# Strassen's seven products for the two bilinear projections: quarters of w_a and w_b, eight of nine token tiles

## The chip, the cores and the metric

The kernel runs on one core of a Trainium2 chip. The metric is the device time of one execution in microseconds (us). The engines are PE (TensorE: matmuls; PEld is its loading of stationary operands), DVE (VectorE), ACT (ScalarE), POOL (GpSimd) and SP (SyncE, which here only issues DMAs). Matmuls read SBUF and write PSUM, eight banks of 128 x 512 fp32.

## The reference

Attention with a forgetting bias is followed by a mixture of eight experts and by a bilinear layer:

```
x = attention(q, k, v, s)                      # 1152 tokens x 512
P = sinkhorn(x @ w_gate)                       # 1152 x 8
y = sum_e P[:, e] * (relu(x @ w1[e]) @ w2[e])  # 512 -> 1024 -> 512, for 8 experts
a = y @ w_a;  b = y @ w_b                      # 512 -> 1536, both
out = (a * b) @ w_out                          # 1536 -> 512
```

Every matmul of the experts and of the bilinear layer is made of three fp16 matmuls: both operands are split into a high and a low fp16 part, and high x high, high x low and low x high are summed in PSUM. The inputs of the bilinear layer's weights come as fp64 and are turned into fp32 on the chip.

## The kernel before, in words

Tokens come in nine tiles of 128, in the order of the list `ORDER`. Attention is interleaved with expert 0. Then experts 1 to 7 follow. For experts 2 to 7 the first product is done by Strassen's scheme with seven products of quarters (`h_seven`): `x_sums` makes four sums of quarters of the activations once, `w_sums` makes the four sums of quarters of the weights for each expert, and the products go through PSUM banks X (`mb` 0 and 1), Y (`yb` 2 and 3), Z (`yb` 4) and A (`mb` 2), with additions on DVE and copies on ACT. The second product of an expert (`y_tile`, lines 1041 to 1043) goes tile by tile, 24 matmuls with 512 moving columns each, into `yb` 0 and 1; DVE adds the result to `acc` (line 1439).

While the experts run, `m2_prep` makes fp16 pairs of the bilinear layer's weights, in pieces of 1 MB of fp64 (18 pieces, six of each weight): a DMA into the tile `mr`, six DVE instructions that turn fp64 into fp32 (lines 1205 to 1213, into `h`), a maximum over the tile (ACT, POOL), then the high part (ACT, line 358) and the low part (DVE, line 372). Two pieces fill one buffer `wun6`, which `m2_out` writes to DRAM. `M2N` says how many such pairs of pieces are made in each expert's stage: 0, 1, 1, 1, 2, 2, 2 for experts 1 to 7. `m2_in` reads the finished buffers back when they are needed.

With the last expert, `xm_split` follows each tile of y: an absolute sum on ACT (line 1452), five small DVE instructions for the scale, the high part on ACT (line 358), the low part on DVE (line 372), and a transposing DMA into `xt` (line 1456). Then come the products with w_a and w_b: `ab_block` takes three tiles (384 columns) at a time, for each of 12 blocks of 128 of the 1536 features and for each of the two weights 12 matmuls (lines 1485 to 1487: four blocks of the 512 inputs by three). ACT copies a with its scale (line 1493), DVE multiplies b into it (line 1496), ACT and DVE split the product into two fp16 parts (lines 1498, 1499). `out_block` makes the last product tile by tile (lines 1525 to 1527). The first `ab_block` stands ahead of the last three tiles of y:

```
for p in range(NTL):
    if last and p == 2 * BT:
        ab_block(0)
    y_tile(e, p, xm_split if last else None)
```

The order of instructions on each engine is made by a list scheduler (`Graph.schedule`) out of written costs, latencies and ranks. Each engine then works through its list in order.

Of the kernel before, what the change touches and what calls it, by code (L numbers as in the profile page):

```python
# [246 lines left out]
def forgetting_attention_moe_bilinear_kernel(  # L247
# [25 lines left out]
    BT = 3  # L273
# [821 lines left out]
    th = []  # L1095

    def switch():
# [8 lines left out]
        for i in range(2):  # L1106
# [4 lines left out]
            big["a", i] = big["ts", i][:, DM:DM + BN]  # L1111
# [3 lines left out]
        for buf, n in ((big["sx"].rearrange("p i z c t -> p (i z c t)"), 3), (big["ht"].rearrange("p z f t -> p (z f t)"), 6)):  # L1115
            for i in range(n):
                th.append(buf[:, i * 8 * BN:(i + 1) * 8 * BN].rearrange("p (z f t) -> p z f t", z=2, f=4))
# [75 lines left out]

    def m2_prep(wi, pc, un, rank):
        if wi < 2:
            a = (w_a, w_b)[wi][:, pc * 256:(pc + 1) * 256]
        else:
            a = w_out[pc * 256:(pc + 1) * 256, :]
        src = a.bitcast(I32).rearrange("(c p) f -> p c f", p=128)
        nch = 4 if wi < 2 else 2  # L1200
# [3 lines left out]
        g.add("SP", 2913, lambda: nc.sync.dma_start(out=stage[2].bitcast(I32).rearrange("p (c f) -> p c f", c=nch), in_=src), r=["hold"], w=sk, rank=rank)  # L1204
# [16 lines left out]
        if wi < 2:  # L1221
            fo = (pc % 2) * 256
            part = lambda zz: units[un][:, zz, :, fo:fo + 256]
            cs = range(4)
        else:
            co = (pc % 2) * 2
            part = lambda zz: units[un][:, zz, co:co + 2]
            cs = range(co, co + 2)
        src2 = cf.rearrange("p (c f) -> p c f", c=nch)
        g.add("ACT", 1145, lambda: hi_of(part(0), src2, sx), r=h0k[1] + [key], w=[("u", un, 0, c, pc % 2) for c in cs], rank=rank)  # L1230
        uk = [("u", un, zz, c) for zz in range(2) for c in range(4)]
        ok = [("u", un, zz, c, pc % 2) for zz in range(2) for c in cs]
# [414 lines left out]
```

## Time and profile before

| | before |
|---|---|
| time, median of 3 runs | 1077.06 us (1074.89 to 1078.08) |
| the profiled execution: its own time | 1076.89 us |
| its span, first to last instruction | 1075.1 us |
| PE busy | 1023.1 us, 95% |
| DVE busy | 655.8 us, 61% |
| ACT busy | 487.8 us, 45% |
| POOL busy | 156.3 us, 15% |

The span is what the trace covers; the execution's own time is 1.8 us longer. A busy share is a mean over stages with different limits, so a change is costed in the stages that it touches. Durations of matmuls overlap (they are pipelined); what a stream of them takes is the step from one start to the next.

### The profile page before, as it was taken

The numbers are of one execution on the slowest core, as the hardware profiler recorded it, in microseconds if no ns is written. First come the engines' busy times: TensorE is split into PE (matmuls) and PEld (weight loads), VectorE is DVE, ScalarE is ACT, GpSimd is POOL, SyncE is SP. The second block draws the span as 40 slices with busy tenths as digits, with TensorE's granted clock in tenths as the row PEclk, the third lists the DMA queues.
The fourth block names the chain that finished last, engine by engine and source line by source line (L and its number), as shares of the span: only waits on it lengthen the run. The fifth ranks groups of instructions, "written<-read, shape, count | busy, mean of one in ns | idle before, by whom it ended". The sixth has DMA issues, their size and how long they took to land.

```text
span 1075.1 us, 18959 instructions
## 1 busy us (share of the span) xinstructions
PE 1023.1 (95%) x7811; PEld 645.8 (60%) x7811; DVE 655.8 (61%) x1361; ACT 487.8 (45%) x920; POOL 156.3 (15%) x192
## 2 busy tenths in 40 slices
PE   1598999999999999999999999999999999999998
PEld 0476777766546745754764774674575564565565
DVE  7885773149975873883793698789668723121221
ACT  4686576246525543652562654553544422021120
POOL 3876666120000000000000000000000000000000
PEclk9899999999999999999999999999999999999999
DMA  9894851011123132221403324413327503100000
GB/s 235 178 184 83 159 81 22 1 51 64 54 79 118 40 118 70 89 71 47 154 4 118 119 64 171 158 40 144 139 110 253 159 1 98 40 1 10 21 1 30
DMA packets 114998, 96.17 MB, mean 89 GB/s; under 512 B 87248, under 2 KB 87504, under 8 KB 112608
## 3 DMA queue, kind: packets, MB, share of 16 engines
q1 hardware_dynamic: 113856, 94.68, 30.3%
q8 instruction: 61, 1.00, 0.4%
q10 hardware_dynamic: 1056, 0.28, 0.1%
q14 instruction: 25, 0.20, 0.1%
HBM read 69.00 MB, written 11.80 MB: 75 GB/s over the span
## 4 chain that ended last, share of the span: by engine, by line
PE 90%; DVE 6%; POOL 2%; issue 1%; DMA 0%; ACT 0%; DVEq 0%; POOLq 0%
PE yb L1041 10%; PE yb L1043 10%; PE yb L1042 10%; PE yb L1381 4%; PE yb L1383 4%; PE yb L1382 4%; PE mb L1485 4%; PE mb L1487 4%; PE mb L1486 4%; PE mb L1381 3%; PE mb L1382 3%; PE mb L1383 3%; PE yb L1526 2%; PE yb L1527 2%; PE yb L1525 2%
## 5 line engine op out<-in xcount | busy, mean ns | idle before, releaser
L1041 PE MATMUL yb<-wun,ht 128*128 128x512 f16 x504 | 191.1, 379 | 0.0
L1042 PE MATMUL yb<-wun,ht 128*128 128x512 f16 x504 | 191.1, 379 | 0.0
L1043 PE MATMUL yb<-wun,ht 128*128 128x512 f16 x504 | 191.1, 379 | 0.0
L1439 DVE SCALAR_TENSOR_TENSOR acc<-yb,pe,acc 128x512 f32<-128x512 f32 x63 | 47.2, 750 | 86.3 <-PE yb L1043 85.0
L358 ACT ACTIVATE wun<-stage,sc 128x1024 f16<-128x1024 f32 (+1 forms) x58 | 60.1, 1054 | 78.4 <-PE yb L1043 71.0
L372 DVE SCALAR_TENSOR_TENSOR wun<-stage,sc,wun 128x1024 f16<-128x1024 f32 (+1 forms) x66 | 80.1, 1231 | 15.7 <-ACT wun L358 15.6
L1043 PEld LDWEIGHTS <-ht 128*128 128x128 f16 x504 | 49.3, 98 | 59.5
L1042 PEld LDWEIGHTS <-ht 128*128 128x128 f16 x504 | 49.3, 98 | 57.3 <-issue 0.3
L1041 PEld LDWEIGHTS <-ht 128*128 128x128 f16 x504 | 49.3, 98 | 57.1
L1381 PE MATMUL yb<-sx,wun 128*128 128x288 f16 x288 | 82.4, 286 | 0.6 <-DVE yb L1396 0.6
L1382 PE MATMUL yb<-sx,wun 128*128 128x288 f16 x288 | 82.4, 286 | 0.0
L1383 PE MATMUL yb<-sx,wun 128*128 128x288 f16 x288 | 82.4, 286 | 0.0
L1382 PEld LDWEIGHTS <-wun 128*128 128x128 f16 x672 | 65.7, 98 | 19.5 <-issue 0.7
L1381 PEld LDWEIGHTS <-wun 128*128 128x128 f16 x672 | 65.7, 98 | 18.8
L1383 PEld LDWEIGHTS <-wun 128*128 128x128 f16 x672 | 65.7, 98 | 16.6
L1496 DVE TENSOR_TENSOR ts<-mb,ts 128x384 f32<-128x384 f32 x36 | 20.1, 557 | 76.8 <-PE mb L1487 76.8
L355 ACT ACTIVATE jk<-stage 128x1024 f16<-128x1024 f32 x52 | 54.7, 1053 | 23.7 <-DMA stage<-in_moe_w_dram 23.2
L1485 PE MATMUL mb<-xt,wun 128*128 128x384 f16 x192 | 62.6, 326 | 0.0
L1487 PE MATMUL mb<-xt,wun 128*128 128x384 f16 x192 | 62.6, 326 | 0.0
L1486 PE MATMUL mb<-xt,wun 128*128 128x384 f16 x192 | 62.6, 326 | 0.0
L897 POOL TENSOR_TENSOR pt<-p,pt 128x512 f16<-128x512 f32 (+1 forms) x46 | 55.0, 1198 | 25.1 <-ACT pt L894 19.8
L1391 ACT ACTIVATE ht<-yb 128x288 f16<-128x288 f32 x96 | 39.0, 407 | 39.1 <-PE yb L1383 37.7
(305 smaller groups left out, 2582.8 us busy)
## 6 DMA issues: line engine op xcount, KB each, us to landing
stage<-in_moe_w_dram SPq DMA_DIRECT2D x26, 1024.0 KB, 5.0
md<-wun SPq DMA_DIRECT2D x9, 1024.0 KB, 3.8
wun<-md SPq DMA_DIRECT2D x7, 1024.0 KB, 6.2
stage<-in_moe_w_dram SPq DMA_DIRECT2D x24, 256.0 KB, 4.3
mr<-in_moe_w_a_dram SPq DMA_DIRECT2D x6, 1024.0 KB, 6.1
mr<-in_moe_w_b_dram SPq DMA_DIRECT2D x6, 1024.0 KB, 5.3
mr<-in_moe_w_out_dram SPq DMA_DIRECT2D x6, 1024.0 KB, 6.0
stage<-md SPq DMA_DIRECT2D x2, 1024.0 KB, 4.8
```

The source lines that it names most:

```text
L358: nc.scalar.activation(hi, src, AF.Copy, scale=scale)
L372: eng.scalar_tensor_tensor(out=lo, in0=src, scalar=scale, in1=hi, op0=ALU.mult, op1=ALU.subtract)
L897: lambda hi=hi, lo=lo, src=src: nc.gpsimd.tensor_tensor(out=lo, in0=src, in1=hi, op=ALU.subtract)),
L1041: nc.tensor.matmul(pp, lhsT=hh, rhs=wh, start=(f == 0), stop=False)
L1042: nc.tensor.matmul(pp, lhsT=hh, rhs=wl, start=False, stop=False)
L1043: nc.tensor.matmul(pp, lhsT=hl, rhs=wh, start=False, stop=(f == KF - 1))
L1381: nc.tensor.matmul(p, lhsT=wh, rhs=xh, start=first and ch == 0, stop=False, skip_group_check=True)
L1382: nc.tensor.matmul(p, lhsT=wh, rhs=xl, start=False, stop=False, skip_group_check=True)
L1383: nc.tensor.matmul(p, lhsT=wl, rhs=xh, start=False, stop=ch == 1, skip_group_check=True)
L1485: nc.tensor.matmul(p, lhsT=wh, rhs=xh, start=(c == 0), stop=False)
L1486: nc.tensor.matmul(p, lhsT=wh, rhs=xl, start=False, stop=False)
L1487: nc.tensor.matmul(p, lhsT=wl, rhs=xh, start=False, stop=(c == KD - 1))
```

## The change

The products with w_a and w_b are regrouped. The 1536 features are handled as six pairs of blocks, j and j + 6. Tile 0 of `ORDER` keeps plain products (`ab_plain`, 128 moving columns). The other eight tiles are two halves of 512 columns, and for each pair of blocks and each weight seven products of quarters stand where there were eight (`ab_seven`). The sums of quarters of the activations are made by `x2_sums` for a tile of each half at a time, into the space of `acc`; the sums of quarters of the weights are made in `m2_prep` beside the quarters themselves, so that a piece of w_a or w_b (one pair of blocks) now fills a whole `wun6`. In DRAM there are 15 such buffers in place of 9. A pair of blocks of w_a and the same of w_b make one entry of the list of preparations (six such entries, then three of w_out), and `M2N` is 0, 2, 1, 2, 1, 2, 1. With the last expert y goes through the tiles in another order, the products with w_a and w_b come behind all of y, and all `out_tile`s behind them.

```diff
@@ m2_prep, for a piece of w_a or w_b
-        g.add("SP", 2913, lambda: nc.sync.dma_start(out=stage[2].bitcast(I32).rearrange("p (c f) -> p c f", c=nch), in_=src), r=["hold"], w=sk, rank=rank)
+            for h in range(2):
+                g.add("SP", 1457, lambda h=h: nc.sync.dma_start(out=dst_()[h], in_=src[h]), r=["hold"] + ([("sth", 0)] if h else []),
...
+            tsum(T[0], qd[:, 0, 1], qd[:, 0, 0])
+            tsum(T[1], qd[:, 1, 1], qd[:, 0, 1])
+            tsum(T[2], qd[:, 1, 1], T[0])
+            tsum(T[3], qd[:, 1, 0], T[2])
+            g.add("ACT", 1145, lambda: hi_of(plain[0](), src2, sx), r=h0k[1] + [key], w=uk(0, 0), rank=rank)
+            g.add("DVE", 1300, lambda: lo_of(nc.vector, plain[1](), src2, sx, plain[0]()), r=h0k[1] + [key] + uk(0, 0), w=uk(1, 0), rank=rank)
+            g.add("ACT", 1145, lambda: hi_of(uv(0)[:, 1024:2048], uf, sx), r=h0k[0] + [key], w=uk(0, 1), rank=rank)
+            g.add("DVE", 1300, lambda: lo_of(nc.vector, uv(1)[:, 1024:2048], uf, sx, uv(0)[:, 1024:2048]), r=h0k[0] + [key] + uk(0, 1), w=uk(1, 1), rank=rank)
...
@@ new: sums of the activations' quarters, for one tile of each half
+    def x2_sums(kk):
...
+        def tt(out, a, b, op, r, w):
+            g.add("DVE", 400, lambda: nc.vector.tensor_tensor(out=out(), in0=a(), in1=b(), op=op), r=r, w=w, rank=rk)
+        def split(i, src, keys):
+            hi, lo = (lambda: accs[:, 4 + kk, i]), (lambda: accs[:, kk, i])
+            g.add("ACT", 400, lambda: nc.scalar.activation(hi(), src(), AF.Copy), r=keys, w=[("S", kk, i, 0)], rank=rk)
+            tt(lo, src, hi, ALU.subtract, keys + [("S", kk, i, 0)], [("S", kk, i, 1)])
...
@@ new: tile 0, plain
+    def ab_plain(j):
...
+                for h in range(2):
+                    p = yb[z][:, h * 128:(h + 1) * 128]
                     for c in range(KD):
...
+                        wh, wl = (wt[:, y, 2 * h + c // 2, c % 2] for y in range(2))
+                        xh, xl = (xt[:, y, c, 0:128] for y in range(2))
...
@@ new: the other eight tiles
+    def ab_seven(j):
+        plain = lambda r, t: (lambda z, c: xt[:, z, 2 * r + c, T0 + t * TN:T0 + (t + 1) * TN])
+        summed = lambda i: (lambda z, c: accs[:, 4 * (1 - z):4 * (1 - z) + 4, i, c])
...
+        for c in range(2):
+            prod(5, c, A, ak, True)
+            act_copy(S5[c], A, ak, [("s5m", c)])
+            prod(1, c, X[c], xbk[c], True)
+            act_copy(Y[c], X[c], xbk[c], yk[c])
+        for c in range(2):
+            prod(2, c, X[c], xbk[c], False)
+            out(c, X[c], xbk[c], 0, 0)
+            prod(6, c, Y[c], yk[c], False)
+            dve_add(Z, Y[c], S5[c], yk[c] + [("s5m", c)], zk)
+            prod(7, c, Y[c], yk[c], False)
+            dve_add(W[c], Y[c], S5[c], yk[c] + [("s5m", c)], [("wm", c)])
+            prod(3, c, Z, zk, False)
+            out(c, Z, zk, 1, 0)
+            prod(4, c, Y[c], yk[c], False)
+            out(c, Y[c], yk[c], 0, 1)
+            out(c, W[c], [("wm", c)], 1, 1)
...
@@ the end of the program
-    m2q = [(wi, x) for wi in range(3) for x in range(NP2 // 2)]
+    m2q = [((0, x), (1, x)) for x in range(FH)] + [((2, x),) for x in range(NP2 // 2)]
...
-        for p in range(NTL):
-            if last and p == 2 * BT:
-                ab_block(0)
+        for p in (0, 1, 5, 2, 6, 3, 7, 4, 8) if last else range(NTL):
             y_tile(e, p, xm_split if last else None)
-    nyb[0] = 5
+            if last and p > 4:
+                x2_sums(p - 5)
...
+    for j in range(3):
+        ab_plain(j)
+    for j in range(3):
+        ab_seven(j)
+        for wi in range(2):
+            m2_in(wi, 3 + j, w2r[wi, j], [], prank())
     for i in range(2):
         m2_in(2, 1 + i, 2 + i, [("u", 2 + i, z, c) for z in range(2) for c in range(4)], prank())
-    out_block(0)
-    ab_block(1)
-    out_block(1)
-    ab_block(2)
-    out_block(2)
+    for j in range(3, FH):
+        ab_plain(j)
+        ab_seven(j)
+    nyb[0] = 5
+    for p in range(NTL):
+        out_tile(p)
...
-M2N = (0, 1, 1, 1, 2, 2, 2)
+M2N = (0, 2, 1, 2, 1, 2, 1)
```

A product (`prod`) is six matmuls of 512 moving columns (two blocks of inputs by three); the index c there is the weight, a or b. For products 3, 5, 6 and 7 the moving operand is read from `accs` as four pieces of 128 columns.

What the scheduler makes of this is seen on DVE at two places. The first is behind the last tile of y of the last expert. Before, DVE has there the addition into `acc` (line 1439), the scale's small instructions and the low part (line 372) that the transposing DMA waits for:

```order
L1439 SCALAR_TENSOR_TENSOR acc_72<-yb1_3545,pe_66,acc_72 128x512
L338 TENSOR_SCALAR sc_63<-sc_63 128x1
L339 TENSOR_SCALAR sc_63<-sc_63 128x1
L342 TENSOR_SCALAR sc_63<-sc_63 128x1
L343 TENSOR_SCALAR sc_63<-sc_63 128x1
L345 TENSOR_SCALAR sc_63<-sc_63 128x1
L1508 TENSOR_SCALAR sc_63<-sc_63 128x1
L372 SCALAR_TENSOR_TENSOR ts1_3537<-acc_72,sc_63,ts1_3537 128x512
```

In the changed kernel the same chain (the addition is line 1451 there, the rest as before) has sums of `x2_sums` for the pair of tiles ahead (line 1496) and the first plain product's multiplication (line 1552) among it; from the addition to the low part:

```order
L1451 SCALAR_TENSOR_TENSOR acc_72<-yb1_3545,pe_66,acc_72 128x512
L1496 TENSOR_TENSOR acc_72<-ts0_3534,acc_72 128x256
L1496 TENSOR_TENSOR ts0_3534<-ts0_3534,ts1_3537 128x256
L338 TENSOR_SCALAR sc_63<-sc_63 128x1
L1496 TENSOR_TENSOR ts1_3537<-xt_71 128x256
L339 TENSOR_SCALAR sc_63<-sc_63 128x1
L1496 TENSOR_TENSOR ts1_3537<-ts1_3537,ts0_3534 128x256
L1552 TENSOR_TENSOR ts0_3534<-yb1_3545,ts0_3534 128x256
L342 TENSOR_SCALAR sc_63<-sc_63 128x1
L343 TENSOR_SCALAR sc_63<-sc_63 128x1
...
L1554 TENSOR_TENSOR sx_3531<-ts0_3534,sx_3531 128x2x128
L372 SCALAR_TENSOR_TENSOR ts0_3534<-acc_72,sc_63,ts0_3534 128x512
```

Eight instructions on 256 columns have moved into the chain (two more of line 1496 stand where the dots are). On PE the first three `ab_plain` (144 matmuls) now stand between the last matmul of y and the first product that reads the last tile's `xt`; before, `out_block(0)` and `ab_block(1)` stood there.

The second place is the change from expert 4's y to expert 5's seven products. Before, DVE has there the low parts of w2 (`wun2`, `wun3`) around the last addition into `acc`, and then the additions and splits of the seven products:

```order
L372 SCALAR_TENSOR_TENSOR wun2_77<-stage0_73,sc_63,wun2_77 128x1024 x2
L1439 SCALAR_TENSOR_TENSOR acc_72<-yb0_3544,pe_66,acc_72 128x512
L372 SCALAR_TENSOR_TENSOR wun3_78<-stage1_74,sc_63,wun3_78 128x1024 x2
L1396 TENSOR_TENSOR yb4_3548<-yb2_3546,s5_0_3535 128x288
L1392 SCALAR_TENSOR_TENSOR ht_3530<-mb0_84,ht_3530 128x288
```

In the changed kernel a piece's preparation ends there (line 1236 is its last subtraction, `wun6` its low parts), and all low parts of w2 come behind:

```order
L1236 TENSOR_TENSOR h0_0_79<-h0_1_80,h0_0_79 128x256
L1451 SCALAR_TENSOR_TENSOR acc_72<-yb0_3544,pe_66,acc_72 128x512
...
L372 SCALAR_TENSOR_TENSOR wun2_77<-stage0_73,sc_63,wun2_77 128x1024
L1408 TENSOR_TENSOR yb4_3548<-yb2_3546,s5_0_3535 128x288
L1404 SCALAR_TENSOR_TENSOR ht_3530<-mb0_84,ht_3530 128x288
L372 SCALAR_TENSOR_TENSOR wun6_3529<-h0_1_80,sc_63,wun6_3529 128x1024
L1408 TENSOR_TENSOR w22_0_3536<-yb2_3546,s5_0_3535 128x288
L1404 SCALAR_TENSOR_TENSOR ht_3530<-mb1_85,ht_3530 128x288
L372 SCALAR_TENSOR_TENSOR wun6_3529<-h0_0_79,sc_63,wun6_3529 128x1024
```

The dots stand for six small instructions on scales. So low parts of 1024 columns stand between the additions that PE's next products wait for.

## Rows read from the trace of the kernel before

**Rows 1.** The page, parts 1, 2 and 4: busy times, granted clock, chain.

```profile
PE 1023.1 (95%) x7811; PEld 645.8 (60%) x7811; DVE 655.8 (61%) x1361; ACT 487.8 (45%) x920; POOL 156.3 (15%) x192
...
PEclk9899999999999999999999999999999999999999
...
PE 90%; DVE 6%; POOL 2%; issue 1%; DMA 0%; ACT 0%; DVEq 0%; POOLq 0%
```

**Rows 2.** Waits of PE from 334 us to the end: total, times, longest.

```profile
PE yb L1381 <- DVE yb L1396: 0.6, 1, 0.6
```

**Rows 3.** Stages by windows: length, busy PE, PEld, DVE, ACT, POOL; clock.

```profile
334.40:422.20 87.80, 87.80 (x555) 54.01 (x553) 58.29 (x108) 42.66 (x81) 2.66 (x4) 1.00 0.25 84
...
597.80:685.60 87.80, 87.80 (x554) 53.99 (x553) 71.14 (x130) 47.20 (x87) 4.31 (x6) 1.00 0.34 121
685.60:773.40 87.80, 87.80 (x555) 53.99 (x553) 71.41 (x130) 47.06 (x87) 4.30 (x6) 1.00 0.33 120
```

**Rows 4.** Groups by line and shape: matmuls with w_a and w_b.

```profile
L1485 PE MATMUL mb<-xt,wun 128*128 128x384 f16 x192 | 62.6, 326 | 0.0
...
L1485 PE MATMUL mb<-xt,stage 128*128 128x384 f16 x96 | 31.3, 326 | 0.0
```

**Rows 5.** PE in order of time: 82 matmuls of 384 columns, 72 of 512.

```profile
879.38 0.33 PE L1487 MATMUL mb<-xt,stage 128*128 128x384 f16 x1
...
892.70 0.38 PE L1041 MATMUL yb<-wun,ht 128*128 128x512 f16 x1
...
908.24 0.38 PE L1525 MATMUL yb<-wun,sx 128*128 128x512 f16 x1
```

**Rows 6.** PE in order of time: 60 matmuls of 128 columns, expert 0.

```profile
203.20 0.22 PE L1021 MATMUL mb<-xt,wun 128*128 128x128 f16 x1
...
206.50 0.22 PE L1023 MATMUL mb<-xt,wun 128*128 128x128 f16 x1
```

**Rows 7.** DVE behind the last tile of y, in order of time.

```profile
908.45 0.75 DVE L1439 SCALAR_TENSOR_TENSOR acc<-yb,pe,acc 128x512 f32<-128x512 f32 x1 [1.45 <-PE yb L1043]
909.99 0.15 DVE L338 TENSOR_SCALAR sc<-sc 128x1 f32<-128x1 f32 x1 [0.79 <-ACT ts L1452]
...
911.43 0.75 DVE L372 SCALAR_TENSOR_TENSOR ts<-acc,sc,ts 128x512 f16<-128x512 f32 x1 [0.41 <-ACT ts L358]
```

**Rows 8.** ACT and SP there: the high part; the last transposing DMA, its landing.

```profile
910.67 0.72 ACT L358 ACTIVATE ts<-acc,sc 128x512 f16<-128x512 f32 x1 [0.72 <-DVE sc L343]
...
912.21 1.24 SPq L1456 DMA_TRANSPOSE xt<-ts  x1
...
DMA to landing us min/median/max: 3.2/3.2/3.2
```

**Rows 9.** All nine transposing DMAs of the last expert: landing.

```profile
DMA to landing us min/median/max: 2.7/3.2/5.0
```

**Rows 10.** Groups by line and shape: narrow additions, copies, high parts, a load.

```profile
L1396 DVE TENSOR_TENSOR yb<-yb,s 128x288 f32<-128x288 f32 x48 | 22.2, 462 | 8.7 <-PE yb L1383 8.7
L1496 DVE TENSOR_TENSOR ts<-mb,ts 128x384 f32<-128x384 f32 x36 | 20.1, 557 | 76.8 <-PE mb L1487 76.8
L1498 ACT ACTIVATE ht<-ts 128x384 f16<-128x384 f32 x24 | 12.5, 522 | 47.4 <-DVE ts L1496 47.4
L358 ACT ACTIVATE wun<-h,sc 128x1024 f16<-128x1024 f32 x18 | 20.6, 1143 | 26.1 <-DVE sc L343 26.1
L1021 PEld LDWEIGHTS <-wun 128*128 128x128 f16 x288 | 28.9, 100 | 0.4
```

**Rows 11.** DVE back to back in order of time, end of expert 6's seven products.

```profile
724.29 1.27 DVE L372 SCALAR_TENSOR_TENSOR wun<-h,sc,wun 128x1024 f16<-128x1024 f32 x1
725.49 0.45 DVE L1392 SCALAR_TENSOR_TENSOR ht<-yb,ht 128x288 f16<-128x288 f32 x1
725.86 0.45 DVE L1392 SCALAR_TENSOR_TENSOR ht<-w,ht 128x288 f16<-128x288 f32 x1
```

**Rows 12.** DMA issues: KB each, median us from issue to landing.

```profile
wun<-md SPq DMA_DIRECT2D x7, 1024.0 KB, 6.2
```

More of the change, by code (lines that the diff above doesn't have):

```diff
@@ L1094, in forgetting_attention_moe_bilinear_kernel @@
     yb = []
-    th = []
     def switch():
@@ new lines, in w_at, with mm @@
+    def w_at(which, j):
+        un = w2r[which, j]
+        wt = lambda: units[un].rearrange("p z a f -> p z (a f)").rearrange("p z (q c f) -> p z q c f", q=8, c=2)
+        return wt, [("u", un, z, c, y) for z in range(2) for c in range(4) for y in range(2)]
+    def ab_plain(j):
+        ab = lambda i: big["ts", i][:, DM + 256:DM + 512]
+        o = j % 2
+        for which in range(2):
+            z = next_yb()
+            wt, wk = w_at(which, j)
+            def mm(z=z, wt=wt):
+                wt = wt()
+                for h in range(2):
+                    p = yb[z][:, h * 128:(h + 1) * 128]
@@ L1516, in out_part @@
-    def out_part(t, ob, j, dst, dkey, wsc, c0, c1):
+            g.add("PE", 24 * 56, mm, r=[("xt", ORDER[0])] + wk, w=[("yb", z)], rank=frank())
+            if which == 0:
+                for h in range(2):
+                    g.add("ACT", 280, lambda z=z, h=h: nc.scalar.activation(ab(o)[:, h * 128:(h + 1) * 128], yb[z][:, h * 128:(h + 1) * 128], AF.Copy,
+                          scale=alpha[:, h * FH + j:h * FH + j + 1]), r=[("yb", z), "alpha"], w=[("ab", o, h)], rank=-5)
+            else:
+                v = lambda: ab(o).rearrange("p (h t) -> p h t", h=2)
+                bk = [("ab", o, h) for h in range(2)]
+                gk = [[gkey(y, j, h, 0) for h in range(2)] for y in range(2)]
+                g.add("DVE", 400, lambda z=z: nc.vector.tensor_tensor(out=ab(o), in0=yb[z][:, 0:256], in1=ab(o), op=ALU.mult), r=[("yb", z)], w=bk, rank=-5)
+                g.add("ACT", 400, lambda: nc.scalar.activation(g_at(0, j, 0, 128), v(), AF.Copy), r=bk, w=gk[0], rank=-5)
+                g.add("DVE", 400, lambda: nc.vector.tensor_tensor(out=g_at(1, j, 0, 128), in0=v(), in1=g_at(0, j, 0, 128), op=ALU.subtract),
+                      r=bk + gk[0], w=gk[1], rank=-5)
@@ L1586, in forgetting_attention_moe_bilinear_kernel @@
                 m2_in(i, 2, 7 + i, [("st", i, c) for c in range(4)], prank())
+            g.add("-", 0, lambda: None, w=sxk + [gkey(z, j, h, p) for z in range(2) for j in range(2) for h in range(2) for p in range(NTL)])
             m2_in(2, 0, 6, [], prank())
```

215 lines of the change are left out of this document (127 added, 88 removed).

## The prediction

> **What bounds the kernel now.** I read the busy times and the chain of waits first. PE is busy for 95% of the span, the chain that ended last is PE's for 90%, and the granted clock stands at the top level in every slice but the first two [rows 1]. Then I asked what PE waited for from expert 2 to the end: one wait of 0.6 us, for DVE [rows 2]. So from 334 us on the kernel is one stream of matmuls, and its length is the number of moving columns times the step from one start to the next. Fewer columns shorten it; any new wait of PE lengthens it. The stages by windows say how much room the other engines have: in a stage of 87.8 us DVE is busy 58.3 us where one pair of pieces of the bilinear weights is prepared, and 71.1 to 71.4 us where two are [rows 3].
>
> **PE's work, removed and added.** Removed are 864 matmuls of 384 columns: 288 on each of three lines [rows 4]. From the first of 82 such matmuls to the next shape are 892.70 - 879.38 = 13.32 us, 0.1624 us a step [rows 5]: 864 x 0.1624 = 140.3 us. Added are 84 products (seven, two weights, six pairs of blocks) of six matmuls with 512 columns: 504. The 72 of that shape take 908.24 - 892.70 = 15.54 us, 0.2158 a step [rows 5]: 108.8 us. Tile 0 adds 288 matmuls of 128 columns. 60 of these take from 203.20 to 206.50 us, 59 steps of 0.0559 us, each with its own load of a stationary operand [rows 6]: 16.1 us. Sum: 108.8 + 16.1 - 140.3 = **-15.4 us**.
>
> The steps of the plain tile are where a rule speaks against the change. In a stream in which each matmul has its own load of weights the trace shows 0.0559 us at 128 columns. The Trainium skill (TensorE: Matmul & The Clock Gate, Back-to-back issue gap) gives about 81 ns a matmul for such a sustained stream at 128 columns; by that figure the plain tile would take 23.3 us and the gain would be 8.2 us, an estimate from that page. The sum goes by the row.
>
> One thing no row shows: a moving operand read as four pieces of 128 columns (products 3, 5, 6, 7: 48 products, 288 matmuls). The nearest rows read 512 columns in one piece, at 0.2158 us a step; four reads of 128 in four matmuls take 4 x 0.0559 = 0.2236 us. So the cost is between 0 and 288 x 0.008 = 2.3 us. I take 0, since a start of a new matmul is more than the step to a new piece.
>
> **The hand-over from y to the products.** Before, the last tile's chain had no one waiting. PE is free of y at 908.24 us [rows 5], DVE's addition starts at 908.45, the low part at 911.43 [rows 7], the transposing DMA at 912.21, and it lands 3.2 us later [rows 8]: 915.4 us, 7.2 us behind PE. Now PE has only three `ab_plain` to cover this: 144 x 0.0559 = 8.0 us. And eight instructions of 256 columns have come into DVE's chain between the addition and the low part. A DVE instruction of 288 columns lasts 0.46 us [rows 10] but follows at a step of 0.37 us back to back [rows 11]; for 256 columns I take 0.34, so 2.7 us. DVE's two waits for ACT in that chain, 0.8 and 0.4 us [rows 7], take up 1.2 us of it, and 1.5 us are left: 7.2 + 1.5 - 8.0 = **+0.7 us** of waiting. Bounds: 0, if more of it fits beside ACT's work (ACT too has new copies there; they lie beside DVE's); and, with no cover at all and the slowest landing of the nine, 5.0 us [rows 9], 7.2 + 8 x 0.46 + 1.8 - 8.0 = 4.7 us.
>
> Behind that wait stand three products with plain operands, 3 x 6 x 0.2158 = 3.9 us. They cover the first sum of the last pair of tiles: three additions and a low part on DVE (4 x 0.34) and a high part on ACT (0.52 at 384 columns [rows 10]), about 2.2 us with the hand-overs; if that cover failed, it would be a wait of up to 2 us. The later sums follow at about 1.5 us each, under 1.3 us of product apiece and with two products more between them; I cost them at nothing.
>
> **The seven products themselves.** The scheme of banks, copies and additions is that of `h_seven`, in which PE lost 0.6 us in six experts [rows 2]. There a product takes six matmuls of 288 columns against an addition of 0.46 us; here six of 512 are 1.29 us, against an addition that I take at 0.70 us (0.46 and 0.56 at 288 and 384 columns [rows 10], so 0.1 us for each 96). In a pair of blocks (18.1 us of these products) ACT has 12 instructions and DVE 12, some 8 us on each. I cost it at nothing; a wait of 0.1 us in each of the six pairs would make 0.6. The weights of pairs 3 to 5 are read into buffers that the first three release, 1 MB in 6.2 us [rows 12], with two pairs' work, 36 us, before them: nothing.
>
> **DVE in the experts' stages.** This is the part that can go wrong. A second pair of pieces costs DVE 71.3 - 58.3 = 13.0 us [rows 3], 6.5 us a piece. A piece of w_a or w_b now has a second low part, 1.20 us back to back [rows 11], and four subtractions of 256 columns, 1.4 us: 9.1 us. Experts 2 and 4 now prepare four such pieces: 58.3 - 13.0 + 36.4 = 81.7 us of 87.8. (At full durations, 1.27 and 0.46, it would be 83.7.) Experts 3 and 5 prepare two (63.5 us), expert 6 as before, expert 7 one pair less. ACT gains one high part of 1.14 us [rows 10] for each piece and stays near 52 us in experts 2 and 4. So DVE is at 93% in two stages, where the most that the trace shows without a wait of PE is 81%. What protects PE: in the order, the low parts of the next expert's weights keep their place ahead of the last three tiles of y, and DVE's lateness falls on the piece's preparation. What doesn't: low parts of 1.2 us now stand between the additions of the first products of expert 5, as of expert 3. I take 0.25 us in each of experts 2 to 5, **+1.0 us**. Bounds: 0; and, if nothing above the 71.4 us fits, 2 x 10.3 = 20.6 us.
>
> **Sum.** 1076.9 (the profiled execution) - 15.4 + 0.7 + 1.0 = 1063.2 us. The median of the runs shown is 0.2 us above that execution, which I leave out. The end of the program, the last product and its two half-width stores, is as before.
>
> **Rivals.**
> - *The hand-over waits longer.* The last transposing DMA goes out just behind a 1 MB read of `wun3`, as before, when it took 3.2 us; the slowest took 5.0. At the upper bound of 4.7 us: 1067.2 us. For it speaks how DVE's chain is stuffed; against it that the chain before had 0.8 us to spare.
> - *DVE binds in part.* Half of what stands above 71.4 us pushes PE out: +10.3 in place of +1.0, 1072.5 us. A quarter: 1067.4.
> - *Slower: DVE binds outright in experts 2 and 4.* All 20.6 us land on PE, since DVE's idle time in a stage is mostly waiting for PE's results and can't be filled: 1082.8 us. It decides from 14.7 us (the gain less the hand-over's wait), 71% of it. Against it: DVE's list is so ordered that the preparation stands in those waits, and in experts 5 and 6 the second pair went into them with no wait of PE.
> - *The plain tile runs slower than the row.* PE would be held by the loads of weights; with the load's recorded length of 0.100 us [rows 10] as the step it would be 288 x 0.044 = 12.7 us more: 1075.9 us. By the page's rule named above it would be +7.2 us, 1070.4. Against both stand the 60 matmuls of expert 0, with the same loads.
> - *That nothing is saved* can be left out: the order holds 504 and 288 matmuls in place of 864.
>
> **How the numbers follow.** My forecast and what lies within 2.5 us of it: 0.65. Longer hand-over: 0.12. DVE in part: 0.12, half of it above 1069 and 0.03 above 1073.8. The plain tile: 0.03, half of it by the load's length. Slower: 0.05. Left over, better than 1060.7: 0.03. From these the range is 1060.7 to 1069.0 us; its lower end is the whole gain with nothing lost (1061.5) and a little for the spread of runs, which is 3.2 us from lowest to highest. A measurement of this kernel can tell 0.3%, 3.2 us. Below 1073.8 us lie the forecast, what is better, the hand-over, 0.09 of DVE in part and half of the plain tile: faster 0.90. Within 3.2 us of the time before: 0.05. Slower: 0.05.
>
> **What the profile of the changed kernel would show.** The steps of matmuls at 0.056 us in `ab_plain` and 0.216 in `ab_seven`, products 3, 5, 6, 7 included; a larger step there is the cost of pieces. From the first `ab_plain` to the last product some 125 us of PE, with one wait of about 0.7 us ahead of the first plain-operand product, released by the transposing DMA. In experts 2 and 4 DVE near 82 us of 87.8, and stages that are no longer than 88.1. If PE shows waits for DVE at the head of experts 3 and 5, or for the low parts of the next weights, the third term was too small; if the stage of experts 2 or 4 grows by 5 us or more, the prediction is wrong.

## The result, and the profile after

The changed kernel takes 1067.8 us (median; 1066.97 to 1067.84), against 1077.09 us for the kernel before on the same chip: a ratio of 0.9912, with a 95% interval of 0.9898 to 0.9925, so 9.3 us or 0.9% faster. (One execution of it was disturbed as a whole and is left out.) The forecast was 1063.2 us. The profiled execution takes 1067.76 us, its span is 1065.9 us, 9.2 us shorter than before.

The page after answers to [rows 1]; its lines are the span, the busy time of each engine, and the clock granted to TensorE in 40 slices:

```profile
span 1065.9 us, 19044 instructions
...
PE 1009.7 (95%) x7739; PEld 626.9 (59%) x7739; DVE 716.6 (67%) x1490; ACT 514.8 (48%) x966; POOL 156.9 (15%) x192
...
PEclk9899999999999999999999999999999999999999
```

PE has 13.4 us less to do, DVE 60.8 us more, the granted clock stays at the top level (2.4 GHz) behind the first two slices. From expert 2 on PE had one wait of 0.6 us before [rows 2]. Now, with the total, the count and the longest behind each:

```profile
PE yb L1393 <- DVE w L1408: 1.9, 2, 1.2
PE yb L1393 <- DVE sc L343: 1.1, 2, 0.6
PE yb L1393 <- DVE yb L1408: 0.9, 2, 0.6
PE mb L1393 <- ACT s L1412: 0.6, 2, 0.3
```

All of them stand at L1393, in the seven products of an expert, not in the new products. The stages answer to [rows 3]. These windows run from the last y of one expert to the last y of the next, experts 2 to 6; the columns are busy time and count on PE, PEld, DVE, ACT and POOL, the granted clock and the DMA engines:

```profile
334.90:423.40 88.50, 88.50 (x559) 54.57 (x558) 75.39 (x140) 45.71 (x88) 4.59 (x6) 1.00 0.38 131
423.40:513.70 90.30, 87.90 (x547) 53.34 (x546) 67.54 (x127) 48.93 (x87) 2.20 (x4) 1.00 0.30 106
513.70:602.20 88.50, 88.50 (x559) 54.55 (x558) 75.55 (x140) 45.71 (x88) 4.59 (x6) 1.00 0.37 131
602.20:691.50 89.30, 87.71 (x548) 53.34 (x547) 67.50 (x127) 48.95 (x87) 2.20 (x4) 1.00 0.30 107
691.50:779.30 87.80, 87.80 (x554) 53.97 (x553) 71.41 (x130) 47.09 (x88) 4.30 (x6) 1.00 0.33 120
```

Experts 2 and 4, which prepare four pieces, lose nothing: PE is busy throughout, and the 0.7 us above 87.8 are products of the next expert taken early. The stages behind them, experts 3 and 5, are where PE stands still.

To add this up I use two measures. A *gap* is the time by which the step from one matmul's start to the next exceeds the usual step of that shape in PE's timeline (steps within 0.02 us of the usual are left out). And *the part from expert 1 on* is the span less the start of expert 1's first y product (L1041). That start lies between 285.1 and 289.2 us in the profiled executions of the table below, ahead of anything edited, so it blurs a time by some 2 us and this part not at all. Before it was 1075.1 - 287.0 = 788.1 us, after 1065.9 - 287.9 = 778.0: 10.1 us less. In it PE's gaps are 0.8 us before (all in expert 7) and 6.3 after: 3.3 at the head of expert 3, 2.2 at the head of expert 5, 0.8 in expert 7. At the hand-over from y to the new products there is none.

**The stall at the head of expert 3.** SP's queue, in DMA issues (start, length, line):

```profile
434.26 0.39 SPq L528 DMA_DIRECT2D stage<-in_moe_w_dram  x1
435.09 0.38 SPq L1206 DMA_DIRECT2D mr<-in_moe_w_a_dram  x1
439.75 0.37 SPq L528 DMA_DIRECT2D stage<-in_moe_w_dram  x1
440.18 0.49 SPq L1206 DMA_DIRECT2D mr<-in_moe_w_a_dram  x1
```

L528 loads the w1 of expert 4, into the two staging buffers that the w2 splits of expert 3 release. In the kernel before, both went out one behind the other at the start of this stage (PE's last y of expert 2 starts at 421.6 us there, at 423.2 in the changed kernel):

```profile
421.88 4.72 SPq L528 DMA_DIRECT2D stage<-in_moe_w_dram  x2
```

Counted from that y, the changed kernel's loads go out 11 to 12 us later. ACT in the same stretch; a bracket is the idle time ahead and what ended it:

```profile
440.79 1.06 ACT L355 ACTIVATE jk<-stage 128x1024 f16<-128x1024 f32 x1 [2.59 <-DMA stage<-in_moe_w_dram]
...
441.84 0.39 ACT L1412 ACTIVATE s<-mb 128x288 f32<-128x288 f32 x1
...
447.24 1.06 ACT L355 ACTIVATE jk<-stage 128x1024 f16<-128x1024 f32 x1 [2.31 <-DMA stage<-in_moe_w_dram]
...
448.29 0.39 ACT L1403 ACTIVATE ht<-yb 128x288 f16<-128x288 f32 x1
```

DVE:

```profile
430.25 1.27 DVE L372 SCALAR_TENSOR_TENSOR wun<-h,sc,wun 128x1024 f16<-128x1024 f32 x1
...
438.41 1.27 DVE L372 SCALAR_TENSOR_TENSOR wun<-stage,sc,wun 128x1024 f16<-128x1024 f32 x1
...
447.25 1.23 DVE L1351 TENSOR_TENSOR ts<-stage,stage 128x1024 f32<-128x1024 f32 x1 [2.76 <-DMA stage<-in_moe_w_dram]
448.39 0.45 DVE L1408 TENSOR_TENSOR w<-yb,s 128x288 f32<-128x288 f32 x1
```

and PE:

```profile
447.36 0.29 PE L1395 MATMUL yb<-sx,wun 128*128 128x288 f16 x1
448.89 0.28 PE L1393 MATMUL yb<-xt,wun 128*128 128x288 f16 x1 [1.25 <-DVE w L1408]
```

Read upwards: PE waits for an addition (L1408), which stands on DVE behind the first subtraction of w1's quarters (L1351), which waits for the load issued at 439.75, which waited for the last low part of the w2 split (438.41), and ahead of the splits stand the low parts of expert 2's last piece (`wun<-h`). DVE is not full when PE waits for it: it stands idle for 2.76 us. The same chain stands at the head of expert 5, with loads at 613.06 and 618.56 us. Not all of the 5.5 us at the two heads is this chain: 0.7 us at each head is a single gap some 10 us further on (460.4 and 638.2 us), where a product waits for an addition that starts as soon as the product ahead of it ends (the list above names L343 for it, but the addition, L1408, ends only 0.05 us before PE goes on). The kernel before has the like of it in expert 7, its only gap of note. So the chain of the loads costs 4.0 us and this hand-back between product and addition 1.4.

**The new products.** PE around the hand-over, one row a matmul:

```profile
867.83 0.22 PE L1539 MATMUL yb<-xt,wun 128*128 128x128 f16 x1
...
875.81 0.22 PE L1541 MATMUL yb<-xt,stage 128*128 128x128 f16 x1
875.87 0.38 PE L1577 MATMUL mb<-xt,wun 128*128 128x512 f16 x1
...
879.53 0.38 PE L1579 MATMUL mb<-xt,wun 128*128 128x512 f16 x1
879.75 0.38 PE L1577 MATMUL mb<-acc,wun 128*128 128x512 f16 x1
...
880.83 0.38 PE L1579 MATMUL mb<-acc,wun 128*128 128x512 f16 x1
```

The 144 matmuls of 128 columns take 8.04 us, 0.0558 a step [rows 6]; the 512-column steps with an operand in one piece (`xt`) and in four (`acc`) are both 0.216 us. The first product starts with no wait at all, and from 867.83 us to the end no step is more than 0.01 us above the usual one.

### The profile page after: what moved, and what is told of

It reads as the page before. It is cut to its first block, busy times and chain, and to the rows that moved or that the text cites. A ratio compares the mean times of both kernels' runs of the same rounds, so it can differ in the third digit from the quotient of the medians.

```text
span 1065.9 us, 19044 instructions
## 1 busy us (share of the span) xinstructions
PE 1009.7 (95%) x7739; PEld 626.9 (59%) x7739; DVE 716.6 (67%) x1490; ACT 514.8 (48%) x966; POOL 156.9 (15%) x192
## 4 chain that ended last, share of the span: by engine, by line
PE 88%; DVE 6%; DMA 2%; issue 1%; POOL 1%; ACT 1%; SPq 0%; DVEq 0%; POOLq 0%; ACTq 0%
PE yb L1041 10%; PE yb L1042 10%; PE yb L1043 10%; PE yb L1393 4%; PE yb L1395 4%; PE yb L1394 4%; PE mb L1393 3%; PE mb L1394 3%; PE mb L1395 3%; PE yb L1647 2%; PE yb L1648 2%; PE yb L1649 2%; PE yb L1578 2%; PE yb L1579 2%; PE yb L1577 2%; DVE wun L372 2%
## 5 line engine op out<-in xcount | busy, mean ns | idle before, releaser
L1041 PE MATMUL yb<-wun,ht 128*128 128x512 f16 x504 | 191.1, 379 | 0.0
L1393 PE MATMUL yb<-sx,wun 128*128 128x288 f16 x288 | 82.4, 286 | 2.0 <-DVE sc L343 1.1
L1041 PEld LDWEIGHTS <-ht 128*128 128x128 f16 x504 | 49.3, 98 | 57.6
L1393 PEld LDWEIGHTS <-wun 128*128 128x128 f16 x672 | 65.7, 98 | 18.4
L355 ACT ACTIVATE jk<-stage 128x1024 f16<-128x1024 f32 x52 | 54.7, 1052 | 37.5 <-DMA stage<-in_moe_w_dram 37.1
L1393 PE MATMUL mb<-xt,wun 128*128 128x288 f16 x192 | 55.0, 286 | 0.0
L1394 PE MATMUL mb<-xt,wun 128*128 128x288 f16 x192 | 55.0, 286 | 0.0
L1395 PE MATMUL mb<-xt,wun 128*128 128x288 f16 x192 | 54.9, 286 | 0.0
L1404 DVE SCALAR_TENSOR_TENSOR ht<-yb,ht 128x288 f16<-128x288 f32 x96 | 43.0, 453 | 17.2 <-ACT ht L1403 16.9
```

Source lines behind the costliest of these rows:

```text
L355: nc.scalar.activation(out, src, AF.Square, accum_out=dst)
L1041: nc.tensor.matmul(pp, lhsT=hh, rhs=wh, start=(f == 0), stop=False)
L1393: nc.tensor.matmul(p, lhsT=wh, rhs=xh, start=first and ch == 0, stop=False, skip_group_check=True)
L1394: nc.tensor.matmul(p, lhsT=wh, rhs=xl, start=False, stop=False, skip_group_check=True)
L1395: nc.tensor.matmul(p, lhsT=wl, rhs=xh, start=False, stop=ch == 1, skip_group_check=True)
L1404: g.add("DVE", 160 + 1.04 * CN, lambda: nc.vector.scalar_tensor_tensor(out=hl(), in0=src(), scalar=0.0, in1=hh(), op0=ALU.max, op1=ALU.sub ...
```

## The experiments

PE's gaps by place, and the part from expert 1 on, of each profiled execution; ratios to the kernel before in the same job.

| kernel | median us | ratio, 95% | from expert 1 on | gaps: expert 3, 4, 5, 6, 7, hand-over | sum |
|---|---|---|---|---|---|
| before | 1077.09 | | 788.1 | 0, 0, 0, 0, 0.8, 0 | 0.8 |
| after | 1067.8 | 0.9912 (0.9898 to 0.9925) | 778.0 | 3.3, 0, 2.2, 0, 0.8, 0 | 6.3 |
| e12_again | 1065.31 | 0.9900 (0.9884 to 0.9916) | 778.2 | 3.5, 0, 2.2, 0, 0.8, 0 | 6.5 |
| e1_old_counts | 1066.04 | 0.9899 (0.9882 to 0.9917) | 778.5 | 0, 1.2, 0, 1.6, 0.2, 3.7 | 6.7 |
| e2_late6 | 1061.78 | 0.9858 (0.9842 to 0.9874) | 773.6 | 0.8, 0, 0.8, 0, 0.1, 0.1 | 1.8 |
| e5_plain_first | 1065.36 | 0.9892 (0.9874 to 0.9909) | 775.8 | 1.1, 0, 2.1, 0, 0.8, 0 | 4.0 |
| e6_three | 1064.53 | 0.9886 (0.9870 to 0.9902) | 775.0 | 0.4, 1.0, 1.1, 0, 0.8, 0 | 3.3 |
| e7_mr_after | 1062.46 | 0.9861 (0.9844 to 0.9878) | 772.8 | 0, 0, 0, 0, 0.8, 0 | 0.8 |
| e10_quarter | 1064.07 | 0.9883 (0.9866 to 0.9899) | 775.6 | 1.0, 0, 2.1, 0, 0.8, 0 | 3.9 |
| e11_both | 1061.75 | 0.9866 (0.9849 to 0.9883) | 773.7 | 0.1, 1.1, 0.7, 0.1, 0.1, 0 | 2.0 |
| e8_spread | 1065.16 | 0.9888 (0.9871 to 0.9906) | 776.6 | 0.8, 2.5, 0.8, 0, 0.8, 0 | 4.9 |
| e9_sums3 | 1064.25 | 0.9879 (0.9864 to 0.9895) | 775.0 | 1.0, 1.2, 0.4, 0.5, 0.1, 0 | 3.3 |
| e13_sums5 | 1081.88 | 1.0052 (1.0039 to 1.0065) | 792.9 | 0.8, 1.3, 0.4, 0.7, 0.3, 17.7 | 21.2 |

The last column accounts for the one on the part from expert 1: with the gaps taken off, the part from expert 1 on is 771.7 to 772.0 us in each of the changed kernels (before: 787.3). So what an edit of the order is worth can be read from the gaps.

**The counts of the kernel before.**

```diff
-M2N = (0, 2, 1, 2, 1, 2, 1)
+M2N = (0, 1, 1, 1, 2, 2, 2)
```

> The changed kernel with the kernel before's list of preparations per expert, 0, 1, 1, 1, 2, 2, 2: only expert 5 (and the last two) prepares two entries in a stage, in place of experts 2, 4 and 6. Theory A (the lost time sits at the heads of experts 3 and 5, behind stages with four pieces: the pieces' last instructions stand ahead of the next w2 splits on DVE and ACT, the staging buffers come free late, the loads of the next w1 land late, and the in-order engines wait for them with the products' copies and additions queued behind): PE's gaps at the heads of experts 3 and 5, 3.3 and 2.2 us, go, and one of 2 to 3 us comes at the head of expert 6: 1064.8 us, 1064 to 1066. Theory B (DVE has too much to do in a stage with four pieces, wherever it stands): the same one stage in place of two, the loss inside expert 5 or just behind it: 1065.1 us. If the lost 6.2 us is elsewhere (in the products with w_a and w_b, or in transfers): 1067.8 us, unchanged.

The gaps at the heads of 3 and 5 are gone and 1.6 us came at the head of expert 6, behind the only stage with four pieces of w_a and w_b. The time hardly moved, since the last pieces now fall into expert 7: PE waits 1.7 us in `ab_plain` for ACT's scaled copy (L1546), whose scales come late, and 3.7 us in all at the hand-over. The place was right, the price not: I had not counted the last expert.

Neither theory has the 1.2 us at the head of expert 4, behind a stage with two pieces. There the w1 loads go out at the start of the stage, as in the kernel before, and DVE still comes to its first use of them too soon, with the addition that PE waits for next in its list:

```profile
509.54 4.72 SPq L528 DMA_DIRECT2D stage<-in_moe_w_dram  x2
...
520.36 1.23 DVE L1351 TENSOR_TENSOR ts<-stage,stage 128x1024 f32<-128x1024 f32 x1 [1.67 <-DMA stage<-in_moe_w_dram]
```

So the stall needs no late release; e11_both has the like at the same place.

**The pieces ranked behind the next expert's splits.**

```diff
-                    m2_prep(wi, pc, 6, prank())
-                m2_out(wi, x, prank())
+                    m2_prep(wi, pc, 6, prank() + 6)
+                m2_out(wi, x, prank() + 6)
```

> The changed kernel with the same pieces in the same stages, but their instructions ranked behind the next expert's w2 splits (6 added to their rank), so that DVE and ACT do the splits that free the staging buffers first, and the pieces' last low parts behind them. The work of each engine is unchanged. Theory A (late release of the staging buffers): the loads of the next w1 go out 5 to 12 us earlier in experts 3 and 5, the waits of ACT and DVE for them go, and PE's gaps of 3.3 and 2.2 us at the heads of experts 3 and 5 go with them: 1062.3 us, 1061.5 to 1063.5. Theory B (too much DVE work in experts 2 and 4): no gain, the gaps move within the stage: 1067.8 us, 1067 to 1069.

1061.78 us; from expert 1 on it is 4.4 us less than in the changed kernel, at unchanged work. SP's queue of this kernel at the head of expert 3:

```profile
423.81 2.76 SPq L528 DMA_DIRECT2D stage<-in_moe_w_dram  x2
```

All of PE's waits in it from expert 1 on:

```profile
PE yb L1393 <- DVE yb L1408: 1.1, 2, 0.6
```

Against the stage's start both w1 loads are out 9 to 12 us sooner, no ACT or DVE instruction at the heads of 3 and 5 waits for a load, and 0.8 us a head is left, nearly all of it the hand-back between an addition and the next product. So of the load chain's 4.0 us 3.8 are gone; expert 7's gap went too. Theory B, the amount of DVE work, falls as the cause of these stalls.

**Three entries in one expert.**

```diff
+M2N = (0, 3, 1, 2, 1, 1, 1)
```

> The changed kernel with three entries (six pieces) in expert 2, two in expert 4, one in each of the others: 0, 3, 1, 2, 1, 1, 1. By the stages of the changed kernel a piece more costs DVE (75.3 - 65.5) / 2 = 4.9 us, so DVE in expert 2 comes to 85 us of 87.8. Theory B (DVE's amount of work binds): the stage of expert 2 or the head of expert 3 grows by 5 to 10 us: 1073 to 1078 us. Theory A (only lateness of the staging buffers counts): expert 3's head loses at most 2 us more than now, expert 5's as now, and the last expert's stages are easier: 1067 to 1070 us.

Not 1073 us, and below what A had foreseen too. The windows of experts 2 and 3 in this kernel:

```profile
334.90:423.40 88.50, 88.50 (x560) 54.57 (x558) 75.92 (x140) 46.25 (x88) 4.48 (x6) 1.00 0.41 143
423.40:511.40 88.00, 87.81 (x551) 53.66 (x550) 79.42 (x148) 46.60 (x83) 3.82 (x6) 1.00 0.33 120
```

DVE has 155.3 us to do in 176.5, against 142.9 in the changed kernel, and PE loses 0.4 us in place of 3.3. And the w1 loads go out still later here, at 446.90 and 465.03. So lateness alone, as I had put A, is wrong too: what matters is where the first user of the load stands in ACT's and DVE's lists. Here DVE's first subtraction (L1351) comes at 471.54 us, ACT's first sum of squares (L355) at 452.28, neither waits, and nothing queues up behind them.

**No load beside w1's** (every load of a piece waits until both w1 loads have landed):

```diff
+        behind = [("st", z, c) for z in wst.get((1, cur[0] + 1), ()) for c in range(4)]
...
-... r=["hold"] + ([("sth", 0)] if h else []),
+... r=["hold"] + behind + ([("sth", 0)] if h else []),
```

> The changed kernel, with each load of a piece of w_a, w_b or w_out waiting until both loads of the next expert's w1 have landed, so that no other load shares the DMA engines with them. Theory C (the loads of w1 land late, 6.9 us in place of 4.7, since half loads of pieces run beside them): the w1 loads land in 4.7 us, ACT's and DVE's waits for them at the heads of experts 3 and 5 shrink by 2 us each and PE's gaps there fall below 2 us in sum: 1064 us, 1063 to 1065.5. Theory A without C (the late release alone): the loads still go out 10 us late and the gaps stay at 3 us or more in sum: 1067 us. A cost of its own may come: SP waits for the landings, and pieces start 5 us later.

The best of all by gaps, 0.8 us, as many as in the kernel before and in the same place, and 1062.46 us. Its w1 loads go out as late as in the changed kernel; SP's queue:

```profile
435.91 5.80 SPq L528 DMA_DIRECT2D stage<-in_moe_w_dram  x2
441.78 1.04 SPq L1209 DMA_DIRECT2D mr<-in_moe_w_a_dram  x2
```

And DVE still waits for them, at the heads of experts 3 and 5 (L1354 there is L1351 of the changed kernel):

```profile
446.44 1.23 DVE L1354 TENSOR_TENSOR ts<-stage,stage 128x1024 f32<-128x1024 f32 x1 [1.21 <-DMA stage<-in_moe_w_dram]
...
622.57 1.22 DVE L1354 TENSOR_TENSOR ts<-stage,stage 128x1024 f32<-128x1024 f32 x1 [1.78 <-DMA stage<-in_moe_w_dram]
```

This edit changes two things at once: what else is in flight, and the places in the lists.

**The same order with a quarter of the pieces' bytes** (of each half load one of four blocks of rows is read):

```diff
-... nc.sync.dma_start(out=dst_()[h], in_=src[h]) ...
+... nc.sync.dma_start(out=dst_()[h][:, 0:1], in_=src[h][:, 0:1]) ...
```

> The changed kernel, with each half load of a piece of w_a and w_b cut to a quarter of its bytes (one of four blocks of rows is read, the rest of the tile is zero), every instruction in its place: only the traffic is smaller. Theory C (the loads of w1 land late since the half loads share the DMA engines with them, and that decides): w1 lands in 4.7 to 5.5 us in place of 6.9, ACT's second wait and DVE's wait at the heads of experts 3 and 5 shrink by 1.5 to 2 us, PE's gaps there fall from 3.3 and 2.2 to 1.0 and 0.9 (the 0.73 that has nothing to do with loads stays): 1064.5 us, 1063.5 to 1066. Theory A alone (late release, whatever else is in flight): the gaps stay at 4 us or more in sum, 1067 us.

Half and half by the gaps, but not for C's reason. DVE at the two heads:

```profile
444.61 1.23 DVE L1351 TENSOR_TENSOR ts<-stage,stage 128x1024 f32<-128x1024 f32 x1 [0.54 <-DMA stage<-in_moe_w_dram]
...
622.51 1.23 DVE L1351 TENSOR_TENSOR ts<-stage,stage 128x1024 f32<-128x1024 f32 x1 [2.79 <-DMA stage<-in_moe_w_dram]
```

At expert 3 the load issued at 439.64 landed in 5.0 us in place of 7.5, and the gaps fell from 3.3 to 1.0. But e5_plain_first (below), which has the changed kernel's order up to there and all the bytes, shows the same: its load is issued at 437.37 us, and DVE has it 5.0 us later, with gaps of 1.1 us.

```profile
442.39 1.23 DVE L1351 TENSOR_TENSOR ts<-stage,stage 128x1024 f32<-128x1024 f32 x1 [0.45 <-DMA stage<-in_moe_w_dram]
```

So the shorter landing cannot be put down to the smaller traffic. At expert 5 the load of 616.14 took 6.4 us with or without the pieces' bytes, and the gaps stayed at 2.1 to 2.2 us. That the traffic beside w1's loads makes the stall (C) is not shown.

What the place does is seen beside e7_mr_after. Counted from PE's last y of expert 4, the data came 22.9 us on here and 22.5 there; PE lost 2.1 us here and nothing there. ACT here, then ACT in e7_mr_after, where the products' copies stand ahead of the first user and not behind it:

```profile
622.57 1.06 ACT L355 ACTIVATE jk<-stage 128x1024 f16<-128x1024 f32 x1 [1.94 <-DMA stage<-in_moe_w_dram]
...
623.63 0.39 ACT L1403 ACTIVATE ht<-yb 128x288 f16<-128x288 f32 x1
```

```profile
622.53 0.41 ACT L1406 ACTIVATE ht<-yb 128x288 f16<-128x288 f32 x1
622.84 1.05 ACT L355 ACTIVATE jk<-stage 128x1024 f16<-128x1024 f32 x1
```

**Both repairs.**

> Both repairs, pieces ranked behind and their loads behind those of w1. If the two are the same loss (late landing of w1 seen by in-order engines), they don't add: 1061 to 1062.5 us, PE's gaps from expert 2 to the end at 1 to 2 us, nearly all at the hand-over and in expert 7. If they were two losses of their own, the gain of 6.0 and of 5.3 us would add to some 1057 us, which PE's work does not allow: 1076.9 - 15.4 = 1061.5 with nothing lost.

1061.75 us: they don't add, so they repair one and the same loss. What is left is not where I had it: 1.1 us at the head of expert 4, 0.7 of expert 5, next to nothing in expert 7.

**The changed kernel once more.**

> The changed kernel once more, to see how far its stalls vary from one execution to the next: 1066.5 to 1068 us; PE's gaps at the heads of experts 3 and 5 between 3 and 5.5 us in sum (in the run with another order of the first products, whose experts are the same, they were 1.1 and 2.2 us; in the profile after, 3.3 and 2.2).

A median 2.5 us lower, from the part ahead of expert 1; the part behind it and the gaps are the same to 0.3 us. The 1.1 us at the head of expert 3 in e5_plain_first, whose order up to there is the same, shows that this stall can be 2 us smaller in another execution: there the load lands in 5.0 us, here in 7.7. A difference of 2 us at that head between two kernels with this order is therefore no effect of an edit.

**Plain products first.**

```diff
         for c in range(2):
-            prod(5, c, A, ak, True)
-            act_copy(S5[c], A, ak, [("s5m", c)])
             prod(1, c, X[c], xbk[c], True)
             act_copy(Y[c], X[c], xbk[c], yk[c])
-        for c in range(2):
             prod(2, c, X[c], xbk[c], False)
             out(c, X[c], xbk[c], 0, 0)
+        for c in range(2):
+            prod(5, c, A, ak, True)
+            act_copy(S5[c], A, ak, [("s5m", c)])
```

> The changed kernel with products 1 and 2 of both weights (plain operands, 4 x 1.29 us) ahead of product 5, the first with a summed operand. My reading of the hand-over (the first products read only columns of tiles that were ready long before, the first sum is 0.64 us late for product 5): one more plain product of 1.3 us covers it, 1067.2 us, with PE's gap of 0.64 us at the hand-over gone. Rival (the sums as a whole are late, and the next products with sums wait in its place): 1067.8 us, the gap moves to product 6, 7 or 3.

Neither was right. Both start from a wait of 0.64 us for the first sum, and the trace of the changed kernel has none: product 5 starts 0.217 us behind the matmul ahead of it, the usual step. There was nothing to cover, and here too no gap stands at the hand-over. The lower time comes from elsewhere (2.4 us from the part ahead of expert 1, 2.2 from the head of expert 3).

**DVE's sums three and five times over** (each piece's four subtractions repeated, on top of e2_late6):

```diff
+            for _ in range(3):
                 tsum(T[0], qd[:, 0, 1], qd[:, 0, 0])
...
```

> The kernel with the pieces ranked behind (1061.8 us), and each piece's four subtractions made three times over, the same result: 8 x 0.33 = 2.7 us of DVE more a piece, 10.7 us more in each of experts 2 and 4, where DVE then has 79 + 10.7 = 89 us against a stage of 87.8, with a part of it running into the next stage as now. If the amount of DVE work binds near there (B): 3 to 8 us more, 1065 to 1070. If DVE's list of a stage can run on into the next one and PE's additions keep their places (A): within 1.5 us of that kernel, 1061 to 1063.5.

> The kernel with the pieces ranked behind (1061.8 us), each piece's subtractions made five times over, 16 x 0.33 = 5.3 us of DVE more a piece and 64 us in all; with three times it was 1064.3 us. DVE from expert 2 to 7 then has some 400 + 64 us of work against 527 us, 88%. If DVE binds outright in full stages (B): 10 us more or above, 1072 or later. If what doesn't fit runs on into the stages behind and only single additions come late (A): 2 to 5 us more than with three times at most, 1066 to 1069.

Three times: 1.4 us more from expert 1 on, 2.5 in the median, between the theories. Five times: 1081.9 us, slower than before, as B's number said, but not where B put it. The experts' stages lose 3.5 us in all; 17.7 us fall at the hand-over. PE's waits of e13_sums5 there:

```profile
PE mb L1578 <- ACT yb L1601: 6.3, 2, 6.1
PE mb L1578 <- ACT acc L1501: 4.5, 1, 4.5
PE mb L1578 <- DMA xt<-ts: 2.1, 1, 2.1
```

The list runs over from stage to stage, and the last piece, of w_out, is prepared between the sums of the activations, when everything is due. Then PE's clock falls as well, as its steps show:

```profile
871.69 0.38 PE L1580 MATMUL mb<-xt,wun 128*128 128x512 f16 x1
878.21 0.59 PE L1578 MATMUL mb<-xt,wun 128*128 128x512 f16 x1 [6.14 <-ACT yb L1601]
878.59 0.63 PE L1579 MATMUL mb<-xt,wun 128*128 128x512 f16 x1
879.01 0.63 PE L1580 MATMUL mb<-xt,wun 128*128 128x512 f16 x1
```

**Entries taken earlier** (`M2N = (0, 2, 2, 2, 1, 1, 1)`, on top of e2_late6):

> The kernel with the pieces ranked behind, and the entries of the list of preparations taken earlier: 0, 2, 2, 2, 1, 1, 1, four pieces in each of experts 2, 3 and 4. Theory A: the order and not the number of stages with four pieces counts: 1062 us, 1061 to 1063.5. Theory B: three full stages in a row, with no easy one behind to take what runs over: 1065 us or more.

B's number, 1065, against A's 1062; 1.7 of the 2.5 us at the head of expert 4 are one gap, behind two full stages in a row. With the pieces ranked behind, full stages in a row do cost something.

**Without the new work on DVE and ACT.**

> The changed kernel without the new work on DVE and ACT for each piece of w_a and w_b: the four subtractions, the second high part and the second low part are left out (the second half of each buffer is set to zero once, so the products with differences of weights are products with zeros). Which stage prepares how many pieces, PE's products and the transfers stay. If the lost time of experts 3 and 5 comes of this new work at all (theories A and B both), PE's gaps there go and the time is 1062 us, 1061 to 1063.5, as with the pieces ranked behind. If the extra transfers (15 buffers written and read in place of 9, two half loads in place of one) make it: 1067 us and the gaps stay.

1064.7 us, a ratio of 0.9878 (0.9858 to 0.9898), between the two times expected. No profile of it can be set beside the others, so it goes by its time alone, blurred by 2 us, and decides little. That the extra transfers make the gaps is excluded by e2_late6, where the transfers are the same and the gaps of the load chain go.

## Why the prediction was right, and where not

**PE's work, -15.4 us: right.** With the gaps taken off, the part from expert 1 on falls from 787.3 to 771.7 us, by 15.6; from before to e7_mr_after, which has the same gaps, it falls by 788.1 - 772.8 = 15.3 us. The steps are those of [rows 5, 6]. The rival of a slower plain tile is out: 0.0558 us a step, with a load of its own for each matmul. The Trainium skill (TensorE: Matmul & The Clock Gate, Back-to-back issue gap) gives about 81 ns for such a sustained stream; the trace does not agree. The operand in four pieces costs nothing.

**The hand-over, +0.7 us: wrong, it is 0, and that by little.** I had the wait ahead of the first plain-operand product, released by the transposing DMA. That product reads none of the last tile's columns: its half is tiles 1 to 4, and the last tile of y lies in the other. It starts at once. What the last tile does hold up is the first sum, which I had costed at nothing. DVE in the profile after:

```profile
877.34 0.76 DVE L1496 TENSOR_TENSOR ts<-xt 128x256 f32<-128x256 f16 x2 [0.85 <-DMA xt<-ts]
...
879.25 0.43 DVE L1496 TENSOR_TENSOR acc<-ts,acc 128x256 f16<-128x256 f32 x1
```

The low part ends at 879.7 us, and product 5 starts at 879.75, without a wait: the 11.9 us of plain work just cover the chain. The chain that answers to [rows 7, 8] took 9.4 us from PE's last y to the landing at 877.27, where I had 7.2 + 1.5 = 8.7; the transposing DMA took 4.2 us in place of 3.2. That the term came out near its forecast is luck: the two errors, a dependency that is not there and a landing 1.0 us later, stand against each other.

**The seven products, 0: right.** Behind the hand-over no step is more than 0.01 us above the usual one.

**DVE in the experts' stages, +1.0 us: the term that was mis-sized; it is 5.5.** These are the gaps at the heads of experts 3 and 5, where before there were none. The work itself I had too high: experts 2 and 3 have 142.9 us of DVE where I had 81.7 + 63.5 = 145.2. The reserve I made for it, 0.25 us in each of four experts, was for additions held up behind low parts of 1.2 us. What came was a longer chain from the same list, 4.0 us: pieces' low parts ahead of the w2 splits, staging buffers free 11 to 12 us late, w1 loads late, and the first users of that load in the lists of ACT and DVE ahead of the products' copies. It takes both, a first user that stands ahead of those copies and data that are not there when the list comes to it: take away the lateness (e2_late6) or the place (e7_mr_after, e6_three), and the chain's gaps go. The other 1.4 us are the hand-back between an addition and the next product, which e2_late6 keeps at both heads and e7_mr_after has at neither. The warning of the prediction, waits for DVE at the heads of experts 3 and 5, is what the profile shows; I had named the sign and not asked what it would cost. Expert 7's 0.8 us was there before.

**Sum.** -15.6 + 0 + 5.5 = -10.1 us, and the part from expert 1 on is 10.1 us shorter. The two spans differ by 9.2, since expert 1 began 0.9 us later. So the forecast was 4.6 us too low by 4.5 of DVE and 0.9 ahead of expert 1, less 0.7 of the hand-over and 0.2 of PE's work. That e12_again, at 1065.3 us, comes nearer to the forecast says nothing for it: the part ahead of expert 1, which the forecast leaves as it was, took 2.9 us less there. Of the rivals, a quarter of "DVE binds in part" gives the nearest time (1067.4), for a reason that e2_late6 and e6_three exclude, and "the hand-over waits longer" the next (1067.2), where no wait is found. "DVE binds outright" exists, but some 60 us of DVE work further on (e13_sums5).

**Left open.** Why a w1 load of the same place lands in 5.0 us in one execution and in 7.5 in another, and why the one at the head of expert 5 takes 6.4 us with little beside it. The DMA view shows a part of it: in the last 1.3 us of the 7.5 (after, expert 3) the engines move at most 33 GB/s, against some 350 before, and in the last 1.4 us of the 6.4 (e10_quarter, expert 5) at most 26; the load of 5.0 us (e5_plain_first) has no such end. What makes this slow end no run shows. Open is also why the hand-back stands where it does. And that the planner puts the first users so early because its written cost of such a load (4 x 728 ns) is less than the 5.0 to 7.7 us measured here is argued from the code, not tried.

## What to carry to other kernels

When work is moved into an engine that has idle time, ask not only whether it fits but what stands behind it in that engine's list, above all instructions that release a buffer: follow the release to the load, and the load to its first in-order user. Here a stall with the engine's name on it, while that engine itself waited for a DMA, was a matter of order; ranking the filler work behind the releases gave back 3.8 of the 4.0 us of the load chain. And a backlog that slides through stages without harm comes due at the one place where its result is needed.

## What the runs showed that I had not expected

- A load of 1 MB for w1 at one and the same place of the list (head of expert 3), with the same half loads of 512 KB issued ahead of it and behind it, landed in 7.5, 7.7 and 5.0 us in three executions (after, e12_again, e5_plain_first).
- In e13_sums5 PE stood still from 872.1 to 878.2 us. Behind that its 512-column steps are 0.427 us in place of 0.216, until 892.3 us with another standstill of some 4.7 us between; the granted clock is 0.50 from 887.5 to 892.3, the lower of the two levels (1.2 GHz), and full again behind it. So that standstill was paid for twice, once by itself and once by slow steps behind it.
- The planner hides filler work well: in e6_three DVE is busy for 88% of two stages with 0.4 us lost between them.
